# A staged float32 kernel (chunked attention and two feed-forward experts): two column pairs of the last product taken in turn, loads spread, due times on one line

## The chip, the cores and the metric

One core of one Trainium2 chip runs the whole kernel. The metric is the device time of one execution in microseconds (us). Of this kernel three executions were timed; one further execution was recorded by the hardware profiler, and every row below is from that one.

The core's engines run their own queues in order: TensorE (PE; its weight loads are PEld), VectorE (DVE), ScalarE (ACT), GpSimd (POOL) and SyncE (SP, which issues all DMAs here). An instruction at the head of a queue that waits holds everything behind it.

## The reference

Attention within chunks of 64 positions, then two experts on the 4608 resulting rows of 512:

```python
# q, k, v: (8, 8, 576, 64); 9 chunks of 64 positions
scores = scale * np.matmul(q_c, k_c.transpose(0, 1, 2, 4, 3))
attn = np.exp(scores - scores.max(-1, keepdims=True)); attn /= attn.sum(-1, keepdims=True) + 1e-09
x = np.matmul(attn, v_c)                    # reordered to (4608, 512)
# first expert: w_in (512, 1024), w_out (1024, 512)
h = x @ w_in
solu = h * softmax(h)
ln = (solu - mu) / np.sqrt(var + 1e-06) * g_ln
y = ln @ w_out
# second expert: w2_in (512, 2048), w2_out (2048, 512)
h = y @ w2_in
return ((h * sigmoid(h)) @ w2_out).astype(np.float32)
```

Activations are float32, the weights float64 (their bits come in as pairs of int32 words).

## The kernel before

Every product is made of three passes over rounded halves (`PASSES`): high x high, high x low, low x high, in the f32r type. A "split" makes the two halves: ScalarE writes the rounded high part, then VectorE or GpSimd subtracts it (L380, L532, L685).

The stages, in order of time:

1. *Tiles* (L753 on), 36 of 128 rows each: q/k load and transpose, scores, softmax, attention times v, first expert in (`moe_in`, L401), its softmax and normalisation, transposes, and by blocks of four tiles the first expert out (`moe_out`, L461; `y_store`, L469). Between them the weights are converted from float64: `conv_load` (L130, one DMA into one of the two places of tag `st_w`), `conv_a` (L143), `conv_b` (L164), `conv_c` (L187), a chain of VectorE steps with one step of ScalarE.
2. *The second expert's way in*, 24 pairs of units of 14 products (`product`, L571; `PA` = 14.588 on the plan). `w2_in` is used in the seven-product form of a 2 x 2 block product: `w2_mix` (L221) makes the seven sums of each block on GpSimd, splits them and stores them (`w2d`); `t_load` (L486) brings the factors back. The results pass through nine places `tmp` (L548) and are stored to `gd` by `g_store` (L583); a place is free again when its store has landed. Meanwhile `w2_out` is converted and mixed in the same way (L867 to L876), into `w2od`.
3. *The way out*, 18 pairs of row tiles, seven products each (`out_product`, L692; 24 matmuls of 256 columns). `w2o_load` (L637) brings the factors in, 512 KB an issue, into places that the way in gives up; `g_load` (L672) brings the four quarters of a pair; `g_sum` (L676: two sums on VectorE, two on GpSimd), `g_split` (L685: ScalarE, then VectorE for the first four, GpSimd for the last three) into a ring of six places, and `o_p1`, `o_sum`, `o_c11` (L705 to L719) combine and store.

Nothing orders itself. Each step is a generator with a list of due times (`Plan.at`, L35), in microseconds of an ideal time line; `Plan.run` (L40) sorts all steps by due time and emits them in that order, so the due times set only the order within each engine's queue. The first tiles have due times written out by hand in the table `LEAD` (L926), in hundredths: up to tile 13 or 14, from -53.24 to 147.93. What isn't in the table has due times by formulas in `T[t]`, the start of tile t (L729), `Z` (last tile), `XO`, `XA` (way in), `XB` (way out) and `SB` = 2.88, one product of the way out. In the table tile 13's first product is due at 139.18; by the formula before, T[13] is 185.9, so the table's steps all come ahead of the formulas'. `conv_load(18)` is the first conversion that isn't in the table; it is due at T[12] - 13.5.

The lines that the steps below touch: L159 and L160 (the two VectorE instructions of `conv_a`), L250 and L252 (high and low part in `w2_mix`), L356 (the softmax product on GpSimd), L391 (VectorE's part of a split, from PSUM), L596 (`u2` of a unit in the way in, VectorE), L610 (`c22`), L674 (`g_load`), L681 (`g_sum`), L688 and L690 (the split of the way out), L710 (`o_sum`). `p2` accumulates on the bank of `p1` and `p7` takes the bank of `p6`, so those products wait for `o_p1` and `u2` of their pair to have read it (`place`, L558). The plan's part for the first pairs of the way out:

```python
for vp in range(NP):
    x = XB + 7 * SB * vp
...
        if vp < 2:
            y = XB + ((-7.5, -6.0, -3.5, -2.0, 3.5, 5.0, 7.0), (11.8, 13.0, 14.8, 17.6, 19.0, 20.3, 23.3))[vp][o]
        at((y, y + 1.25), g_split, vp, o)
        at(x + o * SB, out_product, vp, o)
```

## Time and profile before

| | before |
|---|---|
| time, median of 3 runs | 1358.24 us (1356.92 to 1359.31) |
| the profiled execution: time / span | 1358.2 / 1356.4 us |
| busy share of the span: PE / DVE / ACT / POOL | 94 / 66 / 45 / 42 % |
| mean granted TensorE clock | 0.985 |
| DMA, mean over the span | 160 GB/s, engines busy 57% |

The views used below: *windows* give, for each stretch, the busy time of every engine with its count of instructions, the granted TensorE clock (1.00 is 2.4 GHz, 0.50 would be 1.2 GHz all through), the share of the 16 DMA engines that was busy and the GB/s moved. The *timeline* gives instructions in order of time, neighbours of one line merged (x12 is twelve of them): start, duration, engine, line, operation, output <- inputs and shapes; a bracket tells how long the engine was idle before it and what released it. SPq rows are DMAs being issued. The *chain of waits* goes back from the last instruction. Times in rows are from the start of the span; the plan's due times are on another scale, and only their order and distances count.

### The profile page before, as it was taken

Reading aid. Unit: us, or ns where it says so; the run is one execution under the profiler, and the core shown is the slowest. Engines: PE = TensorE matmul, PEld = TensorE weight load, DVE = VectorE, ACT = ScalarE, POOL = GpSimd, SP = SyncE. Lnnn points to the kernel's source line nnn. Section 1 sums busy time; section 2 is a strip of 40 time slices with the busy share of each in tenths; the row PEclk is TensorE's granted clock in tenths of the full one; section 3 lists DMA queues with packets and bytes.
Section 4 is the critical chain, followed back from the end, with each engine's and each line's share of the span. In section 5 each row is a group of like instructions: output and inputs, shape, how many; then the busy total and the mean of one; then the engine's idle time right before and its main releaser. Section 6 shows DMA issues by size and latency. Waiting matters only on the chain. (4 is left out here: it accounts for less than half of the span.)

```text
span 1356.4 us, 22472 instructions
## 1 busy us (share of the span) xinstructions
PE 1274.6 (94%) x8400; PEld 1166.2 (86%) x8400; DVE 900.7 (66%) x1383; ACT 609.4 (45%) x991; POOL 568.2 (42%) x454
## 2 busy tenths in 40 slices
PE   3789998999999999999999999998889999999998
PEld 2578886887888788788999999988889999999997
DVE  7799785877888788534656656562566666666661
ACT  5686444544544455433545445342333443333341
POOL 4443112321321332322554556252165666676662
PEclk9999999999999999999999999999899999999999
DMA  9574356656555651877676566749973434443420
GB/s 198 93 136 93 68 113 157 134 110 144 140 105 137 148 125 60 289 257 242 199 231 212 184 204 197 216 153 290 334 278 116 145 121 136 135 129 130 134 90 29
DMA packets 330846, 217.51 MB, mean 160 GB/s; under 512 B 187248, under 2 KB 288624, under 8 KB 330736
## 3 DMA queue, kind: packets, MB, share of 16 engines
q1 hardware_dynamic: 330736, 216.07, 56.8%
q8 instruction: 66, 1.08, 0.3%
q14 instruction: 44, 0.36, 0.1%
HBM read 130.03 MB, written 85.98 MB: 159 GB/s over the span
## 5 line engine op out<-in xcount | busy, mean ns | idle before, releaser
L580 PE MATMUL h<-y1s,w2t 128*128 128x384 f32 x1440 | 264.2, 339 | 14.1 <-DVE tmp L596 7.8
L697 PE MATMUL h<-w2o,gs 128*128 128x256 f32 x2160 | 267.3, 284 | 4.4 <-DVE ob L710 3.4
L580 PEld LDWEIGHTS h<-y1s,w2t 128*128 128x128 f32 x1440 | 254.0, 190 | 17.1 <-DVE tmp L596 9.4
L697 PEld LDWEIGHTS h<-w2o,gs 128*128 128x128 f32 x2160 | 263.6, 193 | 4.8 <-DVE ob L710 3.6
L407 PE MATMUL h<-wi,xs 128*128 128x512 f32 x864 | 218.2, 403 | 5.4 <-DVE u L424 2.5
L466 PE MATMUL yp<-lnT,wo 128*128 128x512 f32 x864 | 211.9, 395 | 0.7 <-ACT ys L471 0.7
L407 PEld LDWEIGHTS h<-wi,xs 128*128 128x128 f32 x864 | 162.3, 192 | 42.9 <-ACT e L346 2.9
L466 PEld LDWEIGHTS yp<-lnT,wo 128*128 128x128 f32 x864 | 159.1, 188 | 38.5 <-issue 5.0
L688 ACT ACTIVATE gs<-g 128x1024 fp32r<-128x1024 f32 x117 | 123.4, 1058 | 145.0 <-PE h L697 76.3
L690 POOL TENSOR_TENSOR gs<-g,gs 128x1024 fp32r<-128x1024 f32 x54 | 146.2, 2711 | 51.4 <-ACT gs L688 47.4
L690 DVE TENSOR_TENSOR gs<-g,gs 128x1024 fp32r<-128x1024 f32 x63 | 105.0, 1667 | 33.8 <-ACT gs L688 33.8
L580 PE MATMUL hw<-y1s,w2t 128*128 128x384 f32 x576 | 111.4, 342 | 4.3 <-DVE tmp L610 4.3
L697 PE MATMUL hw<-w2o,gs 128*128 128x256 f32 x864 | 109.7, 282 | 0.9 <-DVE ob L710 0.6
L580 PEld LDWEIGHTS hw<-y1s,w2t 128*128 128x128 f32 x576 | 103.1, 192 | 6.5 <-DVE tmp L610 6.5
L697 PEld LDWEIGHTS hw<-w2o,gs 128*128 128x128 f32 x864 | 105.8, 191 | 1.7 <-DMA w2o<-w2od 0.9
L434 POOL TENSOR_TENSOR st<-st,nhalf 128x1 f32<-128x1 f32 x36 | 21.2, 590 | 197.4 <-DVE st L432 197.4
L237 POOL TENSOR_TENSOR cv<-cv 128x256 f32<-128x256 f32 x64 | 46.1, 737 | 98.4 <-DVE cv L207 97.2
L391 DVE TENSOR_TENSOR lnT<-tp,lnT 128x512 fp32r<-128x512 f32 x72 | 49.4, 686 | 38.7 <-ACT lnT L382 37.9
L681 POOL TENSOR_TENSOR g<-g,g0x 128x1024 f32<-128x1024 f32 x18 | 43.4, 2412 | 74.7 <-DVE gs L690 74.7
L356 POOL TENSOR_TENSOR e<-e,sm 128x512 f32<-128x512 f32 x36 | 42.1, 1170 | 76.5 <-DVE sm L354 69.9
L382 ACT ACTIVATE lnT<-tp 128x512 fp32r<-128x512 f32 x72 | 42.9, 595 | 64.9 <-PE tp L452 64.9
L596 DVE TENSOR_TENSOR tmp<-h,tmp 128x384 f32<-128x384 f32 x48 | 26.6, 556 | 62.0 <-DMA gd<-tmp 26.8
(116 smaller groups left out, 1810.2 us busy)
## 6 DMA issues: line engine op xcount, KB each, us to landing
gd<-tmp SPq DMA_DIRECT2D x192, 192.0 KB
g<-gd SPq DMA_DIRECT2D x72, 512.0 KB
w2d<-cv_m SPq DMA_DIRECT2D x56, 256.0 KB
w2t<-w2d SPq DMA_DIRECT2D x56, 256.0 KB
w2od<-y1s SPq DMA_DIRECT2D x56, 256.0 KB
w2o<-w2od SPq DMA_DIRECT2D x27, 512.0 KB
st_w<-in_moe_w_out_dram SPq DMA_DIRECT2D x24, 512.0 KB
vt<-in_v_dram SPq DMA_DIRECT2D x36, 256.0 KB
```

The source lines that it names most:

```text
L237: nc.gpsimd.tensor_tensor(out=out, in0=in0, in1=in1, op=op)
L356: nc.gpsimd.tensor_tensor(out=e, in0=e, in1=sm.to_broadcast([128, HP, 2, CH]), op=ALU.mult)
L382: nc.scalar.activation(out=hi, in_=src, func=AF.Copy)
L391: nc.vector.tensor_tensor(out=lo, in0=src, in1=hi.bitcast(F32), op=ALU.subtract)
L407: nc.tensor.matmul(h_t[t][:, n, :], xs[:, a, kk, :], wi[b][kk][:, n * 512:(n + 1) * 512], start=(kk == 0 and i == 0), stop=(kk == KD - 1 a ...
L466: nc.tensor.matmul(yps[b, m], wo[a][f // 4][:, f % 4, 128 * m:128 * (m + 1)], lnT[b][c][:, f, :], start=(f == 0 and i == 0), stop=(f == K1 ...
L580: nc.tensor.matmul(acc, w[:, a, kk, :], t[:, i, c, :], start=start and kk == 0 and n == 0, stop=kk == 1 and n == 2, skip_group_check=not s ...
L596: nc.vector.tensor_tensor(out=c, in0=bank[u, "y"], in1=c_t[u, "p1"], op=ALU.add)
L681: on.tensor_tensor(out=out, in0=in0, in1=in1, op=op_)
L688: nc.scalar.activation(out=dst[:, 0], in_=src, func=AF.Copy)
L690: (nc.gpsimd if o > 3 else nc.vector).tensor_tensor(out=dst[:, 1], in0=src, in1=dst[:, 0].bitcast(F32), op=ALU.subtract)
L697: nc.tensor.matmul(acc, g[:, a, f, :], wo2[o, f][:, c, :], start=start and f == 0 and i == 0, stop=f == NF - 1 and i == 2, skip_group_chec ...
```

## The change

The diff does five things. `T[t]` becomes `L * t - 46.7`, so that the formulas and the table lie on one time line and the steps near tiles 12 to 15 interleave. In `w2_mix` of the way in the four parts are spaced 3.6, 6.9, 13.7, 17.4 instead of evenly by 3.8; `t_load` of the `wo` places goes at half the pace. The conversions of `w2_out` get other places, `conv_a` a break between its two VectorE instructions, and their loads are due 7.0 ahead or 5.3 after the piece before. The factors of the way out are loaded at a slower pace in their second to fourth groups, and the fourth starts later. And the first two pairs of the way out take turns: `turn` gives pair 0 the slots 0, 1, 3, 5, 7, 9, 11 and pair 1 the slots 2, 4, 6, 8, 10, 12, 13; ring, loads, sums, splits and stores of these pairs follow new due times, and the places for the results are given by a fixed table.

```diff
-    def conv_a(i):
+    def conv_a(i, apart=False):
...
         nc.vector.tensor_scalar(out=cv[:, 0, :], in0=hi, scalar1=0x7FF00000, scalar2=None, op0=ALU.bitwise_and)
+        if apart:
+            yield
         nc.vector.tensor_scalar(out=cv[:, 1, :], in0=hi, scalar1=0xFFFFF, scalar2=0x100000, op0=ALU.bitwise_and, op1=ALU.bitwise_or)
...
+    def turn(v, o):
+
+        return 7 * v + o if v > 1 else ((0, 1, 3, 5, 7, 9, 11), (2, 4, 6, 8, 10, 12, 13))[v][o]
...
-        dst = ring[(7 * v + o) % 6]
+        dst = ring[turn(v, o) % 6]
...
-        ob.append(ob.pop(0))
-        o_t[v, name] = ob[-1]
-        return ob[-1]
+
+        if v < 2:
+            n = {"p1": (0, 2), "u2": (1, 3), "u3": (4, 0), "c22": (5, 2)}[name][v]
+        else:
+            n = (1, 4, 5, 2, 0, 3)[len(takes) % 6]
+            takes.append(n)
+        o_t[v, name] = ob[n]
+        return ob[n]
...
-    T = [L * t for t in range(TT + 1)]
+    T = [L * t - 46.7 for t in range(TT + 1)]
...
             at(x - 13.5, conv_load, nxt)
+            x = T[t] + (3.6 if nxt == 18 else 0.0)
             at((x + 2.0, x + 2.6), conv_a, nxt)
...
-                    at([y, y + 0.9, y + 1.8, y + 2.7] + [y + 3.6 + 3.8 * (i // 3) + (0.0, 1.0, 2.6)[i % 3] for i in range(12)], w2_mix, (nxt - 17) // 2, 0)
+                    at([y, y + 0.9, y + 1.8, y + 2.7] + [y + (3.6, 6.9, 13.7, 17.4)[i // 3] + (0.0, 1.0, 2.6)[i % 3] for i in range(12)], w2_mix, (nxt - 17) // 2, 0)
...
-        (XA + 0.1, ("wo", "wo")),
-        (XA + 9.0, ("wo", "wo")),
+        (XA + 0.1, ("wo", "wo", "wo", "wo")),
...
-            at([when + (4.4 if tag == "wo" else 0.01) * i + (1.1 if tag == "wo" else 0.001) * k for k in range(n + 1)], t_load, tag, BUFS.get(tag, 2), n)
+            at([when + (8.8 if tag == "wo" else 0.01) * i + (2.2 if tag == "wo" else 0.001) * k for k in range(n + 1)], t_load, tag, BUFS.get(tag, 2), n)
...
-        x = XA + PA * (8 * (i // 6) + ((0.8, 1.4, 2.5, 4.3, 5.5, 6.1) if i < 6 else (0.5, 1.1, 2.2, 2.75, 5.4, 6.0))[i % 6])
-        at(x - 5.0 if i else XA - 1.0, conv_load, n)
-        at((x, x + 1.2), conv_a, n)
-        at((x + 2.4, x + 3.6), conv_b, n)
-        at(x + 4.8, conv_c, n)
+        x = XA + PA * (8 * (i // 6) + ((0.7, 1.4, 2.4, 4.3, 5.4, 6.1) if i < 6 else (0.4, 1.1, 2.2, 2.85, 5.4, 6.1))[i % 6])
+        at(max(x - 7.0, before + 5.3), conv_load, n)
+        before = x
+        at((x, x + 1.0, x + 2.0), conv_a, n, True)
+        at((x + 3.0, x + 4.0), conv_b, n)
+        at(x + 5.0, conv_c, n)
...
         (XB - 2.98 * PA, 1.15, ("wo", "wo", "wo")),
-        (XB - 1.98 * PA, 0.95, ("wo", "u", "u", "wi", "wi", "wi", "wi")),
-        (XB - 13.6, 0.85, ("wi", "wi", "wi", "wi", "xs", "vt", "vt")),
-        (XB + 0.25, 0.55, ("qr", "qr", "kr", "kr", "kT", "pT", "qT", "e")),
+        (XB - 1.98 * PA, 1.4, ("wo", "u", "u", "wi", "wi", "wi", "wi")),
+        (XB - 6.4, 1.5, ("wi", "wi", "wi", "wi", "xs", "vt", "vt")),
+        (XB + 14.7, 0.95, ("qr", "qr", "kr", "kr", "kT", "pT", "qT", "e")),
...
+    FIRST_LOADS = ((-52.5, -52.3, -52.1, -51.9), (-6.0, 2.4, -4.0, 2.1), (18.5, 21.5, 15.0, 17.0))
+    FIRST_SUMS = ((-9.5, -9.0, -3.0, 6.0), (5.4, 6.4, 9.0, 12.0))
+    FIRST_SPLITS = (-7.5, -6.0, 0.0, -2.0, 7.6, 3.0, 9.0, 11.0, 13.6, 15.5, 17.5, 20.0, 22.0, 24.5)
     for vp in range(NP):
         x = XB + 7 * SB * vp
...
+            n = turn(vp, o)
+            y = XB + (FIRST_SPLITS[n] if n < 14 else (n - 4.7) * SB)
             at((y, y + 1.25), g_split, vp, o)
-            at(x + o * SB, out_product, vp, o)
...
+            at(XB + n * SB, out_product, vp, o)
+            ends.append(XB + n * SB + SB)
+        d = 0.6 if vp == NP - 1 else 3.4
...
+        at((ends[4], ends[4] + d), o_sum, vp, "c22", "w", "u3", 1)
```

(The factor groups are due time, time for each 256 KB unit, places; `before` starts at XA - 6.3. Of the loads of `g_load` before, pair 0's were due at -52.5, -49.6, -46.7 and -43.8 from `XB`, pair 1's at 0.3 to 2.4, pair 2's at 11.0 and just after. Some due times of `raw_t` and of the mixing of `w2_out` move by a few us.)

## Rows read from the trace of the kernel before

**Rows 1.** Windows: from:to, length, busy us (instructions) of each engine, clock, DMA share, GB/s
```profile
605.00:617.00 12.00, 12.00 (x71) 12.00 (x70) 6.74 (x13) 4.66 (x10) 0.00 (x0) 1.00 0.94 286
...
925.00:975.00 50.00, 42.55 (x234) 41.57 (x232) 19.69 (x31) 14.42 (x29) 6.15 (x8) 0.97 1.01 344
...
1025.00:1050.00 25.00, 25.00 (x212) 25.00 (x211) 15.74 (x15) 10.09 (x11) 15.97 (x7) 1.00 0.33 111
```

**Rows 2.** The chain of waits: start, us, what; around the way out
```profile
985.04 8.82 DMA g<-gd
...
1102.86 2.88 PE h L697 x24
```

**Rows 3.** Timeline: start, us, engine, line, instruction [idle before, releaser]; the seam
```profile
210.46 1.28 POOL L252 TENSOR_TENSOR cv_m<-cv,cv_m 128x512 fp32r<-128x512 f32 x1
...
219.14 2.91 PE L407 MATMUL h<-wi,xs 128*128 128x512 f32 x12
...
225.81 1.04 SPq L140 DMA_DIRECT2D st_w<-in_moe_w_in_dram  x2
...
230.51 0.43 DVE L159 TENSOR_SCALAR cv<-st_w 128x512 int32<-128x512 int32 x1 [7.57 <-DMA st_w<-in_moe_w_in_dram]
...
233.66 0.68 DVE L391 TENSOR_TENSOR lnT<-tp,lnT 128x512 fp32r<-128x512 f32 x1
...
234.40 1.12 PE L452 MATMUL tp<-ident,u 128*128 128x128 f32 x4 [6.01 <-DVE lnT L391]
...
241.42 2.91 PE L407 MATMUL h<-wi,xs 128*128 128x512 f32 x12
...
256.05 2.91 PE L407 MATMUL h<-wi,xs 128*128 128x512 f32 x12
```

**Rows 4.** Timeline, all engines: tile 18, and the wait of its twin, tile 28
```profile
300.12 2.91 PE L407 MATMUL h<-wi,xs 128*128 128x512 f32 x12
...
307.14 0.42 ACT L250 ACTIVATE cv_m<-cv 128x256 fp32r<-128x256 f32 x1 [4.86 <-DMA w2d<-cv_m]
...
309.42 0.97 PE L362 MATMUL pp<-ident,e 128*128 128x128 f32 x4 [3.23 <-POOL e L356]
...
319.61 2.91 PE L407 MATMUL h<-wi,xs 128*128 128x512 f32 x12
...
459.60 0.97 PE L362 MATMUL pp<-ident,e 128*128 128x128 f32 x4 [2.09 <-POOL e L356]
```

**Rows 5.** Timeline, TensorE: the first pairs of the expert's way in
```profile
623.70 3.88 PE L580 MATMUL h<-y1s,w2t 128*128 128x384 f32 x12 [1.68 <-DVE tmp L596]
```

**Rows 6.** Timeline: the middle of the way in
```profile
764.06 3.84 POOL L517 TENSOR_TENSOR ry<-ry 128x768 f32<-128x768 f32 x2
...
766.12 2.06 DVE L160 TENSOR_SCALAR cv<-st_w 128x512 int32<-128x512 int32 x1
...
896.64 6.00 PE L580 MATMUL h<-y1s,w2t 128*128 128x384 f32 x24 [2.80 <-ACT tmp L592]
```

**Rows 7.** Timeline: the last pairs of the way in
```profile
950.19 0.56 DVE L596 TENSOR_TENSOR tmp<-h,tmp 128x384 f32<-128x384 f32 x1 [6.74 <-DMA gd<-tmp]
...
950.81 1.89 PE L580 MATMUL h<-y1s,w2t 128*128 128x384 f32 x6 [3.84 <-DVE tmp L596]
...
974.94 3.91 PE L580 MATMUL hw<-y1s,w2t 128*128 128x384 f32 x12 [2.47 <-DVE tmp L610]
```

**Rows 8.** Timeline: the first two pairs of the way out
```profile
978.69 11.66 PE L697 MATMUL h<-w2o,gs 128*128 128x256 f32 x96
...
1009.23 3.28 DVE L681 TENSOR_TENSOR g<-g 128x1024 f32<-128x1024 f32 x1 [4.48 <-DMA g<-gd]
...
1014.16 5.49 PE L697 MATMUL h<-w2o,gs 128*128 128x256 f32 x24 [3.42 <-DVE ob L710]
```

**Rows 9.** Costliest groups: line, engine, shapes, count | busy us, mean ns | idle before
```profile
L688 ACT ACTIVATE gs<-g 128x1024 fp32r<-128x1024 f32 x117 | 123.4, 1058 | 145.0 <-PE h L697 76.3
...
L690 DVE TENSOR_TENSOR gs<-g,gs 128x1024 fp32r<-128x1024 f32 x63 | 105.0, 1667 | 33.8 <-ACT gs L688 33.8
```

More of the change, by code (lines that the diff above doesn't have):

```diff
@@ L634, in chunk_attention_moe_moe @@
     NP = TT // 2
-    wo2, wu, ring, raw_g, op, ob, o_t = {}, [], [], {}, {}, [], {}
+    wo2, wu, ring, raw_g, ob, takes, o_t = {}, [], [], {}, [], [], {}
     def w2o_load(tag, bufs, n):
@@ L657, in g_places @@
         elif n == 4:
-            for i in (2, 3):
+            for i in (0, 2):
                 raw_g[1, i] = sb.tile([128, NF, 128], F32, tag="cv", name="g1", bufs=2)
         elif n == 5:
-            for i, tag in ((0, "cv_s"), (1, "cv_s"), (4, "st_w")):
+            for i, tag in ((3, "cv_s"), (1, "cv_s"), (4, "st_w")):
                 raw_g[1, i] = sb.tile([128, NF, 128], F32, tag=tag, name="g1", bufs=2)
@@ L693, in out_product @@
         acc, start = place(1000 + v, SEVEN[o], 256)
-        g = ring[(7 * v + o) % 6]
+        g = ring[turn(v, o) % 6]
         for f in range(NF):
@@ L898, in chunk_attention_moe_moe @@
         for i in (2, 3, 0, 1):
[L899 to L900 removed]
+            at(XB + FIRST_LOADS[vp][i] if vp < 3 else x - 11 * SB + 0.1 * i, g_load, vp, i)
         for n in range(4):
[L902 to L905 removed]
+            at(XB + FIRST_SUMS[vp][n] if vp < 2 else x + (-6.2, -5.7, -3.2, -0.9)[n] * SB, g_sum, vp, n)
+        ends = []
         for o in range(7):
[L907 to L909 removed]
+            n = turn(vp, o)
+            y = XB + (FIRST_SPLITS[n] if n < 14 else (n - 4.7) * SB)
             at((y, y + 1.25), g_split, vp, o)
[L911 to L919 removed]
+            at(XB + n * SB, out_product, vp, o)
+            ends.append(XB + n * SB + SB)
+        d = 0.6 if vp == NP - 1 else 3.4
+        at(ends[0], o_p1, vp)
+        at(ends[1], o_sum, vp, "u2", "y", "p1", 1)
+        at((ends[2], ends[2] + d), o_c11, vp)
+        at(ends[3], o_sum, vp, "u3", "y", "u2", 1)
+        at((ends[4], ends[4] + d), o_sum, vp, "c22", "w", "u3", 1)
+        at((ends[5], ends[5] + d), o_sum, vp, "c21", "v", "u3", 0)
+        at((ends[6], ends[6] + d), o_sum, vp, "c12", "w", "u2", 0)
     with tc.manual_schedule(engines={ET.PE, ET.SP, ET.Activation, ET.DVE, ET.Pool}):
```

24 lines of the change are left out of this document (4 added, 20 removed).

## Prediction

> **What bounds the kernel now.** I read the engines' busy time first (the table above): TensorE is busy 94% of the span, so only its idle time and its slow-clock time can be won. Then the windows: in the steady way out TensorE works in every microsecond, 212 matmuls in 25 us at a granted clock of 1.00 [rows 1]; nothing can be gained there. Then the timeline of TensorE alone for each wait above 0.3 us, and the other engines around each. A wait costs its own length and, where the clock fell from 2.4 to 1.2 GHz in it, the extra time of the next matmuls. Full speed is 0.169 us for a matmul of 384 columns (71 in 12.00 us) and 2.88 us for 24 of 256 [rows 1, 2]. After the first 100 us, where no queue's order changes, the losses lie in six places:
>
> (a) The seam, where the hand-written lead table ends. Tile 13 starts at 219.14, tile 14 at 241.42: 22.28 us, where the next takes 14.63. Loss 7.6. VectorE stood 7.57 us at `conv_a(18)`, whose load SyncE issued only at 225.81; the split that frees the transposes' bank queued behind it, and TensorE waited 6.01 [rows 3].
> (b) Tiles 18 and 28, each after an odd tile with a `w2_mix`, whose stores queue on SyncE behind the q/k loads. ScalarE stood 4.86 us for such a store to land, GpSimd's subtraction behind it, and the softmax product behind that on GpSimd; TensorE waited 3.23 and the tile took 19.49, 4.9 too many. The twin's wait was 2.09; with the same slow clock (4.86 - 3.23) that is 3.7. Loss 8.6 [rows 4].
> (c) The start of the expert's way in: two waits of this kind (one row stands), 1.52 and 1.68, with 0.3 and 1.9 of slow clock. Loss 5.4 [rows 5].
> (d) Its middle: two waits of one shape (the second stands), 1.65 and 2.80, with 0.4 and 1.9 of slow clock. Loss 6.8 [rows 6].
> (e) Its end: the 50 us from 925 hold 234 matmuls, 39.5 us of work, so 10.5 are lost, and 1.9 more to the slow clock after 974.94. Loss 12.4 [rows 1, 7].
> (f) The first pairs of the way out: ten products take 35.5 us (978.69 to 1014.16) instead of 28.8, with a wait of 3.42 at the end, and the next one 5.49 instead of 2.88 by the slow clock. Loss 9.3 [rows 2, 8].
>
> That is 50 us in all.
>
> **The change part by part.** No arithmetic is added or removed and all 8400 matmuls stay; TensorE's own order changes only in the first 14 products of the way out. What moves is the place of other instructions in their queues.
>
> *One time line (a).* T is 46.7 less, so `conv_load(18)` falls at 111.4, inside the lead table, some 28 places earlier on SyncE, and `conv_a(18)` at 130.5. The load's place is free after `conv_b(16)`, due at 116.0; until 119.2 nothing else is due on SyncE, so holding that queue costs nothing. But `conv_a(18)` also needs the `cv` that the second part of `w2_mix(0)` leaves at 211.74, and its chain, 3.15 us from the first instruction to the split behind it, then sits ahead of that tile's split, transposes and maximum instead of in an empty stretch [rows 3]. ScalarE and TensorE wait for those. I take 3 us lost where 7.6 were (0 to 5): gain 4.6 (2.6 to 7.6). `load_qk(9)` now stands ahead of a `y_store` on SyncE; the two places of `ys` cover the delay, a tile's length.
>
> *Parts of `w2_mix` (b).* The third part moves 2.5 later, its subtraction behind GpSimd's softmax product, which is due 0.9 after the old place and 1.6 before the new. ScalarE still waits until about 307, but TensorE then has the next half of its tile to do. Gain 7.5 (0 to 8.6).
>
> *`t_load` of the last 16 factors (c).* 16 x 256 KB come in 35 us instead of 17.6, 119 GB/s instead of 238, in a stretch that ran at 286 [rows 1]. The stores whose landing frees `tmp` get through sooner. The last factor is due 33.1 into the stage and first used at about 57. Gain 4 (1 to 5.4).
>
> *Conversions of `w2_out` (d).* Half of the loads go out 7.0 instead of 5.0 ahead of their use, the others 4.2 to 4.9, and `conv_a`'s two instructions have places apart. In both waits VectorE stood for the load and then worked beside GpSimd's two subtractions: L160 took 2.06, where its sister L159 takes 0.43 alone [rows 3, 6]. Now `c21` goes ahead of the two and `c12` soon behind, so what is left delays neither for long. I take 5 of 6.8 (1 to 6.8). The Trainium skill, SBUF — State Buffer, section Who interferes with whom, says that such a VectorE instruction and a GpSimd one shut each other out fully. The rows agree: 2.06 ends as the second subtraction does. By that rule each of the two, now apart, could be held up for 1.9, the gain would be 3, and the sum 2 us later.
>
> *Loads before the way out (e).* By the diff's due times, 512 KB a load: the second group left each 1.9 us (276 GB/s), now each 2.8 (187); the third each 1.7 (308), now each 3.0 (175). The `gd` stores add eight of 192 KB in 14.6 us, 108. So the demand falls from 384 and 416 to 295 and 283, where the DMA engines, all busy, moved 344 [rows 1]. The `gd` store for which VectorE stood 6.74 us lands sooner, and TensorE's 3.84 and 0.9 go [rows 7]. The wait at 974.94 is VectorE's own work for the first splits; GpSimd's first sum stands 2 later and may halve it. Against it, the first pair's four loads leave in one burst at -52.5: 2.1 MB at 344 GB/s hold the queue for 6 us, which can cost 0 to 4; I take 1.5. Gain 6 (1 to 10).
>
> *Two pairs in turn (f).* Pair 0 has slots 0, 1, 3, 5, 7, 9, 11, pair 1 has 2, 4, 6, 8, 10, 12, 13. The last factor is first used at 31.7 instead of 17.3. The old wait goes: VectorE's first sum of pair 2 stood 4.48 us for its load ahead of `u2` of pair 1, which is now due 8 earlier than that sum [rows 8]. A new one comes: slot 4 needs pair 1's sums and so its a22. That load follows the store of `c12(47)`, as the old one did; then it began 6.3 after the stage and took 8.82 [rows 2]; now perhaps 4.0, and 4.7 as the pair of loads at 225.81 did [rows 3]. Two sums, ScalarE's pass and VectorE's take 3 x 1.67 + 1.06 = 6.1 [rows 9]. Slot 4 is ready between 14.8 and 21.2 against 11.5, or up to 2 sooner where VectorE isn't held up: a wait of 1 to 10, taken as 3, with 2.6 of slow clock. It shifts the later slots alike and is paid once. Gain 9.3 - 5.6 = 3.7 (-3 to 8). Output stores leave 2.8 later; the six `ob` places leave 8 us before one is needed again.
>
> Sum: 4.6 + 7.5 + 4 + 5 + 6 + 3.7 = 30.8; the low ends sum to 3, the high ones to 46. The profiled execution took 1358.2 (its span 1356.4 and 1.8 around it), which is the median of the runs, so 1358.2 - 30.8 = **1327**.
>
> **Rivals.** *Only the tiles.* The queue still carries, from plan time -7.3 to 11.6 around the start of the way out, six factor loads, four of products and six stores: 6.4 MB in 18.9 us, 340 GB/s, as much as the 344 of the full stretch [rows 1]. If it stays full, (e) and (f) give nothing together and (c) and (d) half: 4.6 + 7.5 + 4.5 = 16.6, 1342. For it: that demand; against: the 30 us before it are well below. The Trainium skill, DMA: Bandwidth & Descriptors, section Specifications, gives some 358 GB/s of HBM for one core; by it 340 would just pass.
>
> *All of it.* (a) and (b) whole, (c) and (d) whole, (e) 10, (f) 8: 46, 1312. For it: each wait was released by an instruction that the diff moves. Against: the late a22.
>
> *The turns starve* (slower). With two pairs open at once, every slot from 4 to 13 waits for its split, as GpSimd falls behind and SyncE holds the last factor loads behind a load that waits for one of its splits. A wait like that at 1014.16 costs 3.42 + 2.6 = 6.0 [rows 8]; ten cost 60 where 9.3 were lost: 1358 - 27 - 9 + 60 = 1382. It makes the kernel slower from seven of the ten slots on. Against it: in the steady pairs GpSimd is busy 15.97 of 25 us [rows 1].
>
> *No change.* The dues move, but landing times set (b) to (f) all the same; then only what is left of (a) stays, within 2.7 us: 1356.
>
> **How the numbers follow.** Forecast (1317 to 1337): 0.62. Only the tiles (1337 to 1352): 0.18. All of it (1306 to 1317): 0.10. No change: 0.04. Starved: 0.06. The range leaves out the last two, half of "all of it" and the far end of "only the tiles": 1314 to 1346. A measurement of this kernel tells about 0.2%, 2.7 us, from no change: faster 0.90, the same 0.04, slower 0.06.
>
> **What would show it.** After: no stand of VectorE for the load of `conv_a(18)`, tile 13 under 18 us; no wait for the softmax product in tiles 18 and 28; no 6 us stand for a `gd` store in the last pairs of the way in; the way out within 370 us, with one wait, at its fifth product. Wrong would be: waits at several of the first fourteen products, one above 5 us in the lead table's last tiles, or a stop some 45 us before the way out, after the four loads in one burst.

## The result, and the profile after

The changed kernel takes 1346.97 us (median of four runs, 1344.13 to 1347.89) against 1358.66 (1356.92 to 1359.31) for the one before in the same comparison: a ratio of 0.9912, 95% interval 0.9895 to 0.9930. That is 11.7 us faster where I had forecast 31, and 1 us above the range. The profiled execution's span is 1345.2 us (1356.4 before), and the spans' difference, 11.2, can be laid out by stage from the first matmul of each:

| stretch | before, us | after, us | gain | predicted |
|---|---|---|---|---|
| up to tile 11's first product | 189.91 | 190.67 | -0.8 | 0 |
| (a) tiles 11 to 14 | 66.14 | 62.00 | 4.1 | 4.6 |
| (b) tile 15 to the way in | 343.17 | 337.24 | 5.9 | 7.5 |
| (c), (d), (e) the way in | 379.47 | 375.36 | 4.1 | 15 |
| (f) the way out | 370.96 | 373.35 | -2.4 | 3.7 |
| what follows | 6.75 | 6.59 | 0.2 | 0 |

So the tiles did nearly what I said, the way in a quarter of it, and the way out the opposite. The way in can be counted by its 24 pairs: a pair is 84 matmuls, which at 0.173 us each (twelve in 2.08 us where TensorE works through) take 14.56 us, and what it takes beyond that is lost. The first four pairs, (c), lost 6.6 before and lose 8.8 now; the 17 behind them, (d), 11.9 and 6.3; the last three, (e), 11.5 and 10.9.

The timeline of TensorE alone shows where. Columns as in [rows 3]; line numbers of the changed kernel are 2 larger than before from the second instruction of `conv_a` to `g_sum`, and 6 to 11 larger behind it (L582 is the way in's matmul, L703 the way out's).

```profile
222.54 3.27 PE L409 MATMUL h<-wi,xs 128*128 128x512 f32 x12 [0.85 <-DVE u L426]
238.10 2.91 PE L409 MATMUL h<-wi,xs 128*128 128x512 f32 x12
...
297.00 2.91 PE L409 MATMUL h<-wi,xs 128*128 128x512 f32 x12
...
312.36 3.26 PE L409 MATMUL h<-wi,xs 128*128 128x512 f32 x12 [0.22 <-DVE u L426]
...
466.47 0.66 PE L364 MATMUL pp<-ident,e 128*128 128x128 f32 x4 [0.35 <-POOL e L358]
...
613.35 3.58 PE L582 MATMUL h<-y1s,w2t 128*128 128x384 f32 x12 [2.44 <-DVE tmp L598]
...
632.78 1.32 PE L582 MATMUL h<-y1s,w2t 128*128 128x384 f32 x6 [1.89 <-DVE tmp L598]
...
639.99 2.37 PE L582 MATMUL hw<-y1s,w2t 128*128 128x384 f32 x12 [1.70 <-DVE tmp L612]
...
937.70 2.29 PE L582 MATMUL h<-y1s,w2t 128*128 128x384 f32 x6 [4.88 <-DVE tmp L598]
...
961.73 3.75 PE L582 MATMUL hw<-y1s,w2t 128*128 128x384 f32 x12 [2.08 <-DVE tmp L612]
...
980.03 11.33 PE L703 MATMUL h<-w2o,gs 128*128 128x256 f32 x70 [2.04 <-DVE gs L696]
...
1005.10 1.34 PE L703 MATMUL hw<-w2o,gs 128*128 128x256 f32 x9 [0.86 <-DMA w2o<-w2od]
1009.08 0.62 PE L703 MATMUL hw<-w2o,gs 128*128 128x256 f32 x3 [2.64 <-DMA w2o<-w2od]
1009.54 4.52 PE L703 MATMUL h<-w2o,gs 128*128 128x256 f32 x24
```

Against [rows 3, 4]: tile 13 now takes 15.56 us (222.54 to 238.10) where it took 22.28, tile 18 takes 15.36 (297.00 to 312.36) where it took 19.49, and the twin's wait is 0.35 where it was 2.09. Against [rows 5]: the start of the way in still stops, now three times. Against [rows 7]: the wait for VectorE's `u2` near the end is not gone but longer, 4.88 for 3.84. Against [rows 8]: the old wait at 1014.16 is gone, and in its place stand the one that I had forecast at the fifth product (980.03) and two for factors, which I had not.

### The profile page after: what moved, and what is told of

It is laid out like the page before. It is cut to its first block, busy times and chain, and to the rows that moved or that the text cites. A ratio compares the mean times of both kernels' runs of the same rounds, so it can differ in the third digit from the quotient of the medians.

```text
span 1345.2 us, 22475 instructions
## 1 busy us (share of the span) xinstructions
PE 1271.6 (95%) x8400; PEld 1162.0 (86%) x8400; DVE 898.2 (67%) x1383; ACT 609.7 (45%) x991; POOL 567.1 (42%) x454
## 3 DMA queue, kind: packets, MB, share of 16 engines
q8 instruction: 66, 1.08, 0.3%
## 5 line engine op out<-in xcount | busy, mean ns | idle before, releaser
L703 PE MATMUL h<-w2o,gs 128*128 128x256 f32 x2160 | 269.4, 286 | 2.5 <-DVE gs L696 2.0
L582 PE MATMUL h<-y1s,w2t 128*128 128x384 f32 x1440 | 261.6, 337 | 9.9 <-DVE tmp L598 9.2
L703 PEld LDWEIGHTS h<-w2o,gs 128*128 128x128 f32 x2160 | 265.8, 194 | 3.1 <-DVE gs L696 2.2
L582 PEld LDWEIGHTS h<-y1s,w2t 128*128 128x128 f32 x1440 | 252.4, 189 | 11.8 <-DVE tmp L598 10.4
L409 PEld LDWEIGHTS h<-wi,xs 128*128 128x128 f32 x864 | 159.4, 190 | 45.8 <-issue 3.2
L582 PE MATMUL hw<-y1s,w2t 128*128 128x384 f32 x576 | 111.6, 343 | 6.8 <-DVE tmp L612 6.8
L703 PE MATMUL hw<-w2o,gs 128*128 128x256 f32 x864 | 109.2, 282 | 3.5 <-DMA w2o<-w2od 3.5
L582 PEld LDWEIGHTS hw<-y1s,w2t 128*128 128x128 f32 x576 | 103.3, 193 | 9.1 <-DVE tmp L612 9.1
L703 PEld LDWEIGHTS hw<-w2o,gs 128*128 128x128 f32 x864 | 105.5, 191 | 3.9 <-DMA w2o<-w2od 3.9
L598 DVE TENSOR_TENSOR tmp<-h,tmp 128x384 f32<-128x384 f32 x48 | 26.6, 556 | 63.1 <-DMA gd<-tmp 34.7
```

The lines of the kernel that those rows point to most:

```text
L409: nc.tensor.matmul(h_t[t][:, n, :], xs[:, a, kk, :], wi[b][kk][:, n * 512:(n + 1) * 512], start=(kk == 0 and i == 0), stop=(kk == KD - 1 a ...
L582: nc.tensor.matmul(acc, w[:, a, kk, :], t[:, i, c, :], start=start and kk == 0 and n == 0, stop=kk == 1 and n == 2, skip_group_check=not s ...
L598: nc.vector.tensor_tensor(out=c, in0=bank[u, "y"], in1=c_t[u, "p1"], op=ALU.add)
L703: nc.tensor.matmul(acc, g[:, a, f, :], wo2[o, f][:, c, :], start=start and f == 0 and i == 0, stop=f == NF - 1 and i == 2, skip_group_chec ...
```

## What held VectorE and SyncE

The waits of the way in, seen from VectorE and SyncE's queue (a timeline of the changed kernel, both ends of the stage; L598 is `u2`, L590 a store of `tmp` to `gd`, L257 a store of the mixing of `w2_out`):

```profile
606.93 0.38 SPq L140 DMA_DIRECT2D st_w<-in_moe_w_out_dram  x1
607.40 0.40 SPq L590 DMA_DIRECT2D gd<-tmp  x1
...
612.74 1.02 DVE L598 TENSOR_TENSOR tmp<-h,tmp 128x384 f32<-128x384 f32 x2 [5.81 <-DMA gd<-tmp]
...
626.35 1.00 SPq L590 DMA_DIRECT2D gd<-tmp  x2
...
632.17 0.56 DVE L598 TENSOR_TENSOR tmp<-h,tmp 128x384 f32<-128x384 f32 x1 [4.82 <-DMA gd<-tmp]
...
927.99 0.32 SPq L257 DMA_DIRECT2D w2od<-y1s  x1
928.40 0.96 SPq L590 DMA_DIRECT2D gd<-tmp  x2
...
930.30 1.88 SPq L590 DMA_DIRECT2D gd<-tmp  x3
...
937.09 0.56 DVE L598 TENSOR_TENSOR tmp<-h,tmp 128x384 f32<-128x384 f32 x1 [7.78 <-DMA gd<-tmp]
```

Each of these three waits is for a store that had only just been issued: 607.40 to 612.7, 626.35 to 632.2, and 931.64 (the third of the three merged at 930.30) to 937.1, so 5.3 to 5.8 us of landing. (The start's third stop, 1.70 at 639.99, is of another kind: VectorE's conversion came late behind a mixing step of GpSimd, which had stood 7.66 for a store of the mixing.) Which store it is follows from `take`. There are nine places and each pair of units takes eight, handed round in the order of taking. So `u2` of a pair's second unit gets the place that `u2` of the first unit held in the pair before, and that one is given up late, by the store of `c12`: on the plan 4.0 us earlier. In the second pair, where two of the nine places have joined the list late, `u2` of the first unit gets a place whose store was due 2 us earlier. No pace of the loads gives such a store more than 4 us to land. In my prediction I never asked how long the order of the places leaves for it.

In the way out (timeline of VectorE and SyncE, then the chain of waits, then a window with columns as in [rows 1]):

```profile
973.65 1.23 DVE L683 TENSOR_TENSOR g<-g,g 128x1024 f32<-128x1024 f32 x1 [1.73 <-DMA g<-gd]
...
979.90 0.64 SPq L734 DMA_DIRECT2D out_dram<-ob  x1
985.93 0.33 SPq L676 DMA_DIRECT2D g<-gd  x1
986.35 0.38 SPq L646 DMA_DIRECT2D w2o<-w2od  x1
```
```profile
999.26 9.77 DMA w2o<-w2od
```
```profile
980.00:985.00 5.00, 4.97 (x23) 4.97 (x24) 1.11 (x1) 1.85 (x3) 3.81 (x2) 0.50 0.14 45
```

From 980.54 to 985.93 SyncE issued nothing, and the DMA engines moved 45 GB/s: its next instruction was pair 2's load into a place that a split of pair 0, on GpSimd until about that time, still read. The last seven issues of factors stood behind it and its three fellows; the last landed at 1009.03, in the middle of the twelfth product.

## The experiments

In all of them the kernel before, in the same comparison, took 1355.8 to 1358.6 us. A kernel's time moved by several us between runs there, so I read mostly the stages' lengths in the traces, one for each kernel. They have a spread of their own: four kernels whose instructions in the way in stand in the same order (the changed one, `factors_first`, `split_stores` and, but for one load and the last pair, `turns_undone`) took 375.4, 374.9, 376.5 and 372.7 us for it, and three with the same way out (the changed one, `conv_undone`, `old_pace`) 373.4, 374.4 and 374.8. The table has them all; "tiles" is tile 11's first product to the way in.

| kernel | time, us (range) | tiles | way in | way out |
|---|---|---|---|---|
| before | 1358.66 | 409.3 | 379.5 | 371.0 |
| changed | 1346.97 | 399.2 | 375.4 | 373.4 |
| tiles_only | 1349.65 (1345.56-1356.63) | 398.9 | 383.0 | 370.4 |
| places_released | 1336.68 (1335.78-1338.46) | 399.0 | 365.5 | 375.6 |
| factors_first | 1342.39 (1340.16-1344.95) | 398.5 | 374.9 | 369.4 |
| turns_undone | 1341.85 (1339.34-1342.25) | 398.9 | 372.7 | 369.3 |
| released_old_pace | 1333.20 (1330.40-1334.77) | 398.6 | 361.2 | 376.1 |
| conv_undone | 1353.71 (1350.54-1355.97) | 399.1 | 381.6 | 374.4 |
| factor_pace_undone | 1345.87 (1344.43-1346.51) | 398.2 | 378.7 | 368.7 |
| released_in_order | 1332.91 (1329.82-1334.63) | 398.5 | 363.0 | 370.1 |
| old_pace | 1345.67 (1343.87-1346.08) | 398.3 | 373.9 | 374.8 |
| all_mended | 1326.18 (1323.53-1326.33) | 398.9 | 360.2 | 369.3 |
| later_turns | 1331.87 (1331.10-1333.21) | 398.9 | 362.7 | 373.1 |
| in_order_mended | 1326.67 (1324.74-1330.21) | 398.5 | 359.6 | 368.3 |
| later_mended | 1324.64 (1323.47-1326.32) | 398.9 | 361.4 | 367.1 |
| later_early_stores | 1327.99 (1326.26-1332.22) | 398.6 | 361.4 | 370.2 |
| split_stores | 1337.13 (1336.73-1337.44) | 398.5 | 376.5 | 367.1 |
| later_split | 1320.26 (1318.15-1322.38) | 399.0 | 361.2 | 363.9 |
| in_order_split | 1322.99 (1322.12-1324.35) | 398.7 | 361.8 | 367.6 |

**The tiles alone.** The kernel before with `T` shifted by 46.7, 3.6 on `conv_a(18)`, and the new spacing of `w2_mix`.

> The kernel before with the tile part of the change alone: the one time line for T, conv_a(18) 3.6 later, and the new spacing of w2_mix's four parts. Theory (each part of the change pays for itself): read from the two traces, the changed kernel gains 4.1 us at the seam and 5.9 in the tiles behind it, 10.1 in all, so this should take 1358.4 - 10.1 = 1348, and the way in and the way out should last as before, 379.5 and 371.0 us. Rival (the later parts are coupled to the tiles, since the tiles' last steps shift the loads of the way in): the way in alone changes by more than 2 us and the time lies outside 1346 to 1350.

Ratio 0.9946 (0.9924 to 0.9968). The tiles take 398.9 us, so (a) and (b) stand by themselves, 10.4 us. But the way in took 383.0, 3.6 more than before, which the rival had, though the time stays inside its 1346 to 1350. Part of it is the clock after the stop at the start (granted 0.72 and 0.94 in the twenty us from 608.84, 0.83 and 1.00 in the same twenty of before), 1.3 a wait of 1.85 at 805.36 which was 0.52. Both were there before, only shorter. The way in has its instructions in the same order in both kernels, and 3.6 is no more than the four kernels above differ by, so a coupling to the tiles is not shown.

**The order of the places.** In the way in, a place goes to the end of the list when it is stored:

```diff
     def take():
-        tmp.append(tmp.pop(0))
-        return tmp[-1]
+        return tmp.pop(0)
...
         nc.sync.dma_start(out=gd[...], in_=c.rearrange("p (t c) -> p t c", c=128))
+        tmp.append(c)
```

> The changed kernel, but a place tmp of the way in goes back to the end of the list when its store is issued, not when it is taken. With nine places and eight taken in each pair of units, the order of taking gives u2 of the second unit the place whose c12 store was due 4.0 us before on the plan, and in the second pair, where two places come late, u2 gets one whose store was due 2 us before; the order of release leaves at least 8 us for every place. Theory (the waits at the start and the end of the way in, 2.44, 1.89 and 4.88 with 2.3 and 1.5 of slow clock, are the short time that this order leaves for a store to land, and loads at another pace can't take them away): all three go or shrink below 0.5, and the time falls by 9 to 12 us, to 1335 to 1338. Rival (the DMA queue is full in these stretches and VectorE waits for it whatever the place): the waits stay, at other products, and the time is within 3 us of the changed kernel's 1347.

The way in fell by 9.8 us to 365.5 and the kernel to 0.9854 (0.9827 to 0.9881) of before, as the theory had it: the waits of 2.44, 1.89 and 4.88 are gone. By the count of pairs 8.5 of the 9.8 come from the last three pairs (2.4 lost where 10.9 were) and only 1.6 from the first four (7.2 where 8.8 were). Timeline of VectorE (line numbers in the way in are one smaller here), and windows, of the end of its way in:

```profile
928.46 0.56 DVE L598 TENSOR_TENSOR tmp<-h,tmp 128x384 f32<-128x384 f32 x1 [2.40 <-DMA gd<-tmp]
```
```profile
922.00:927.00 5.00, 5.00 (x31) 5.00 (x30) 1.58 (x3) 1.86 (x4) 1.14 (x2) 1.00 1.01 345
927.00:932.00 5.00, 5.00 (x30) 5.00 (x29) 1.28 (x3) 0.99 (x2) 0.00 (x0) 1.00 1.08 293
```

The DMA engines are as full as in the changed kernel (1.01 and 1.08) and TensorE works through: the queue was not the cause, the time left for the store was. VectorE still stands 2.40 for a store, which costs nothing now. One stop at the start grew, from 1.70 to 3.90 (timeline of the same kernel): VectorE's conversion waits for a mixing step of GpSimd, and that for a store of the mixing to land.

```profile
627.86 0.40 POOL L250 CAST y1s<-cv 128x256 fp32r<-128x256 f32 x1 [7.69 <-DMA w2od<-y1s]
...
629.11 0.59 DVE L159 TENSOR_SCALAR cv<-st_w 128x512 int32<-128x512 int32 x1 [6.92 <-POOL y1s L254]
...
633.83 2.61 PE L581 MATMUL hw<-y1s,w2t 128*128 128x384 f32 x7 [3.90 <-DVE tmp L612]
```

**The pace of the last 16 factors**, first on top of that, then alone; both have `("wo", "wo")` at `XA + 0.1` and at `XA + 9.0` and 1.1 us a unit again.

> The kernel with the places in the order of release, and the last 16 factors of the way in (t_load into wo) at the pace of the kernel before, 1.1 a unit in two groups. In the kernel at the slow pace one wait is left at the start of the way in: 3.90 at 633.83, where VectorE's conv_a had stood 6.92 for a mixing step of GpSimd, which stood 7.69 for a store of w2od to land. Theory (the slow pace drags the factor loads into the stretch from 618 to 632, where the mixing's stores, raw_load's four loads and a conversion's load are on the queue too; the pace was the wrong thing to change): that wait falls below 1, nothing takes its place, and the way in takes 360 to 362 us instead of 365.5. Rival (the stretch is full at either pace): the way in takes 364 to 368.

> The changed kernel with t_load's last 16 factors at the pace of the kernel before; nothing else. My prediction gave this pace 4 us. Theory (at the start of the way in the order of the places sets the stop, and the pace only moves it from the first pairs to the third): the start loses 5.5 to 8.5 us at either pace, and the way in takes within 2.5 us of the 375.4, 374.9 and 372.7 of the three kernels with the slow pace. Rival (my prediction): without the slow pace the way in takes 378 to 380.

With the places mended the old pace is better by 4.3 us (way in 361.2): the stop at 633.83 shrinks to 1.98, though not below 1. With the places as they are the pace changes nothing: 373.9 against 372.7 to 376.5, with waits of 1.60, 1.94, 0.76 and 1.01 in place of 2.44, 1.89 and 1.70. So the slow pace of the change is at best worth nothing.

**The conversions of w2_out**, due as before, loads and mixing too.

> The changed kernel with the conversions of w2_out as in the kernel before: due times of the loads, of conv_a to conv_c and of the mixing, and conv_a's two instructions together. Theory (my prediction's step for the middle of the way in, 5 us, was right: the two traces show 10.0 of waits and slow clock there before and 4.8 after): waits of 1.6 to 2.9 at p1 of the pair come back twice in the middle, and the way in takes 379 to 382 us instead of 375.4. Rival (the middle was freed by what happens ahead of it, not by these due times): the way in stays within 1.5 us of 375.4.

The way in took 381.6, 6.3 more, nearly all of it in the middle (12.5 lost there where 6.3 were), with the two waits of [rows 6] back at the same places (TensorE's timeline; 1.65 and 2.80 before):

```profile
769.38 4.46 PE L582 MATMUL h<-y1s,w2t 128*128 128x384 f32 x24 [1.59 <-ACT tmp L594]
...
893.84 6.00 PE L582 MATMUL h<-y1s,w2t 128*128 128x384 f32 x24 [2.87 <-ACT tmp L594]
```

**The pairs in order, and the factors' pace at the end of the way in.** `turns_undone` has `turn` as `7 * v + o` and the due times, places and last two factor groups of before; `factor_pace_undone` has in addition

```diff
-        (XB - 1.98 * PA, 1.4, ("wo", "u", "u", "wi", "wi", "wi", "wi")),
+        (XB - 1.98 * PA, 0.95, ("wo", "u", "u", "wi", "wi", "wi", "wi")),
...
-            y = XB + FIRST_LOADS[0][0] if vp == 0 else ...
+            y = XB - (3.6 - 0.2 * i) * PA if vp == 0 else ...
```

> The changed kernel with the first two pairs of the way out one after the other, as in the kernel before: their slots, sums, splits, loads and places, and the third and fourth group of factors, as before; pair 0's loads in one burst, the second group's slow pace and all that is ahead of the way out stay changed. Theory (the turns cost more than they bring, since the last factors land too late): the way out takes 371 us as before, and the kernel 2 us less than the changed one, 1345. Rival (my prediction: the turns bring some 4 us by themselves): 1350 to 1352.

> The changed kernel with its way out in order (as the kernel turns_undone), and in addition the second group of w2_out's factors at the old pace (0.95 a unit) and pair 0's four loads 2.9 us apart as before. With that the end of the way in is as it was before the change. Theory (the stop there is the 4.0 us that the order of the places leaves for c12's store to land, and the queue is full at either pace): the wait for u2 of the second unit, 3.46 in turns_undone, stays between 2.5 and 5, and the way in takes 372 to 375 us against 372.7 there. Rival (my prediction: the pace is worth 6 us): 377 to 380 us.

In order, the way out takes 369.3, 4.0 less than with the turns: as built, with the late factors that came with them, they cost 4 us. The pace together with the burst of pair 0's loads is worth 6.0 against `turns_undone` (378.7 and 372.7), as I had said, and there my later theory missed. But against the other three of that order it is only 2.2 to 3.8, and in the last three pairs alone, where the edit acts, 13.8 are lost against 9.2 to 10.9. The wait for `u2` (TensorE's timelines, `factor_pace_undone`, then `turns_undone`):

```profile
938.50 2.29 PE L582 MATMUL h<-y1s,w2t 128*128 128x384 f32 x6 [6.64 <-DVE tmp L598]
```
```profile
934.16 1.32 PE L582 MATMUL h<-y1s,w2t 128*128 128x384 f32 x6 [3.46 <-DVE tmp L598]
```

The slower pace does land the store sooner; with 4.0 us on the plan that isn't soon enough.

**The factors ahead of pair 2's loads.**

```diff
-        (XB + 14.7, 0.95, ("qr", "qr", "kr", "kr", "kT", "pT", "qT", "e")),
+        (XB + 4.0, 0.75, ("qr", "qr", "kr", "kr", "kT", "pT", "qT", "e")),
```

> The changed kernel, but the last group of w2_out's factors (qr to e, 14 units) is due at XB + 4.0 in steps of 0.75 instead of XB + 14.7 in steps of 0.95, so that SyncE issues all of it ahead of the loads of pair 2. Theory (SyncE stood until 985.93 for the place of pair 2's load, which a split of pair 0 reads, and held the factor loads behind it; the last of them landed at 1009.03): the waits of 0.86 and 2.64 in the twelfth product and their slow clock go, 5 us, and the way out takes 368 us instead of 373; 1342. Rival (the DMA engines can't bring 3.5 MB more before then, and the transfers collide): the same wait stands at another product or for pair 2's loads, the way out takes 372 to 375 us, 1347.

The waits for factors went, and the way out takes 369.4, 3.9 less. A new one came, for an `ob` place whose store took 10.73 us to land (chain of waits, TensorE's timeline, and a window in those 10.73):

```profile
1004.68 10.73 DMA out_dram<-ob
```
```profile
1015.96 5.99 PE L703 MATMUL h<-w2o,gs 128*128 128x256 f32 x48 [2.31 <-ACT ob L717]
```
```profile
1008.00:1010.00 2.00, 2.00 (x19) 2.00 (x18) 2.00 (x3) 0.93 (x1) 2.00 (x1) 1.00 0.14 48
```

The engines were nearly idle while it took so long: 0.14 busy, 48 GB/s. This comes back below.

**Together, with and without turns.** `released_in_order` joins the release order and the pairs in order; `all_mended` joins release order, old pace, factors first and `(5, 4, 2, 1, 0, 3)` for the `ob` places; `in_order_mended` joins release order, old pace, the pairs in order, and `(-4.6, -4.2, -3.2, -0.9)` for pair 2's sums.

> The changed kernel with the places of the way in in the order of release and the way out in order. If the two gains are independent, the way in takes 365.5 us less some 2 (turns_undone's was 2.6 shorter than the changed kernel's, by its third group of factors) and the way out 369.3: 1331 us. If the earlier end of the way in only moves the wait for the factors (the way out of places_released was 2.3 longer than that of the changed kernel), the way out takes 372 and the kernel 1334.

> The changed kernel with places in the order of release, t_load at the old pace, the last factor group ahead of pair 2's loads, and the ob places handed on in the order in which the first two pairs free them (5, 4, 2, 1, 0, 3). If the terms add up: the way in takes 361 us (released_old_pace), the way out 366 to 369 (369.4 in factors_first less its wait of 2.31 for an ob place; one wait of 2 and its slow clock left at the fifth product), the kernel 1325. If the end of the way in, now 14 us earlier against the loads, lacks the transfers (released_old_pace's way out took 376.1), waits for w2o stay and the way out takes 371 to 375: 1329 or more.

> Places in the order of release, t_load at the old pace, the way out in order with its old due times but for VectorE's two sums of pair 2, which are due 4.6 us later, behind u2 of pair 1. Theory (in order, the loss at the eleventh product is VectorE standing for pair 2's load ahead of u2): that wait (2.21 in released_in_order) goes with its slow clock, what is left is the wait for the last factors (2.87), and the way out takes 366 to 368 us, the kernel 1325 to 1328. It also tells whether turns are needed at all: if all_mended is not faster than this, taking turns brought nothing that a sum in another place doesn't bring.

`released_in_order` lies between its two cases, way out 370.1, with a wait of 2.87 for factors at 972.90: an end of the way in that comes earlier meets the factors earlier. `all_mended` and `in_order_mended` end level, 0.9768 (0.9751 to 0.9785) and 0.9781 (0.9759 to 0.9802) of before, both 1.3 to 1.5% faster than the changed kernel. In the first, the fifth product waits 3.33 and 1.73, and its chain of waits says why (then TensorE's timeline):

```profile
947.04 7.27 DMA gd<-tmp
...
954.37 5.46 DMA g<-gd
```
```profile
963.69 0.80 PE L703 MATMUL h<-w2o,gs 128*128 128x256 f32 x2 [3.33 <-ACT gs L694]
```

The way in's last store must land before pair 1's load of it may go: 12.7 us for the two, and the slot begins about 11.5 after the start of the way out.

**Pair 1 two slots later.** `turn` as `((0, 1, 2, 3, 5, 7, 9), (4, 6, 8, 10, 11, 12, 13))` with sums and splits to match; then the same with its new waits taken away, and once more with early stores. (In `later_turns` a sum of pair 1 runs ahead of the split that still reads its place, so one low half is made from the wrong numbers, by the same instructions; the two others have it in the right order.)

> As all_mended, but pair 1 comes in later: pair 0 has the slots 0, 1, 2, 3, 5, 7, 9, pair 1 the slots 4, 6, 8, 10 to 13; sums and splits are due accordingly. Theory (the wait at the fifth product is the turns' own: pair 1's p6 needs a22, whose load can only follow c12's last store): the wait goes, the way out takes 4 to 5 us less than in all_mended, 363 to 365, and the kernel 1321. Rival (the last factors are needed two slots sooner, at the tenth product, and aren't there): a wait for w2o of 2 to 4 us takes its place, and the way out is as long as all_mended's.

> As later_turns, with three things set right: the second sum of GpSimd for pair 1 stands behind the split that reads its a12 (in later_turns it ran ahead of it, so that one low half was made from the wrong numbers, with the same instructions); c22 of pair 1 takes the ob place that c22 of pair 0 left, not the one whose store of c11 was 8.6 us old (7.08 lost there); VectorE's two sums of pair 2 are due behind c22 of pair 0 (2.47 lost there). Theory (taking turns can bring what I predicted, once loads, places and sums leave it room): no wait above 1 us in the first fourteen products, the way out takes 363 to 365 us against 369.3 in all_mended and 368.3 in in_order_mended, and the kernel 1320 to 1322. Rival (the transfers themselves set the end of the first pairs): the wait comes back as one for w2o or for g, the way out takes 367 to 371, 1324 to 1328.

> As later_mended, with the stores of out due 0.6 behind their sums as in the kernel before, instead of 3.4. Theory (a store issued early lands early, and SyncE holds nothing behind it for long, since the loads of the steady pairs need not go out before them): the way out is within 1 us of later_mended's. Rival (SyncE stands for each store's sum, and the loads queued behind it come later): 1 to 4 us more, with waits for g in the pairs 2 and 3.

The wait at the fifth slot went in all three, and no wait for factors came. `later_turns` lost 2.47 to VectorE's sums of pair 2 and 7.08 to an `ob` place; `later_mended` got rid of both, only to wait 3.80 in the twelfth product for pair 2's loads, which now land late behind the factors (its chain of waits, and TensorE's timeline):

```profile
961.37 10.55 DMA w2o<-w2od
...
971.98 8.96 DMA g<-gd
```
```profile
984.90 4.50 PE L703 MATMUL hw<-w2o,gs 128*128 128x256 f32 x24 [3.80 <-DVE ob L721]
```

Its DMA engines moved 304, 369, 417, 398 and 364 GB/s in the five windows of 5 us from 955, busy all through. So the rival seemed to hold: the way out, 367.1, is inside its 367 to 371, and only 1.1 below the pairs in order. Early stores moved the wait to 6.40 and the way out to 370.2, as their rival had it: the change's later stores are worth 3 us where two pairs are open.

**The stores to out.** Left open was why an `ob` place came back so late. `o_store` issues one transfer for two batch rows; here it is two, one for each:

```diff
-        nc.sync.dma_start(out=out...[2 * tt:2 * tt + 2, b * CH:(b + 1) * CH, 256 * n:256 * n + 256], in_=c)
+        rows = out.rearrange("(b s) f -> b s f", b=B)
+        for h in range(2):
+            nc.sync.dma_start(out=rows[2 * tt + h, b * CH:(b + 1) * CH, 256 * n:256 * n + 256], in_=c[CH * h:CH * h + CH])
```

> factors_first, with each store to out issued as two, one for each of its two batch rows (64 partitions, 64 KB). In factors_first the first result of pair 2 waited for a place whose store took 10.73 us, while the DMA engines were 0.14 busy and moved 48 GB/s for 8 us: not behind loads, but behind other stores, four of 128 KB. Theory (a store over two batch rows is cut in two and uses 2 of 16 engines; 0.14 x 16 = 2.2): cut along its 64 rows instead, a store goes over all engines, the windows without loads no longer stand at 48 GB/s, the wait of 2.31 at 1015.96 goes with its slow clock of 0.2, and the way out takes 366 to 367.5 us against 369.4. Rival (rows of 1 KB written to memory go at 48 GB/s however they are cut): the window and the wait stay, 369 to 370.

> later_mended with the stores to out split in the same way. If the stores' engines matter to the loads in flight too (two engines carry the stores and their share of each load, so a load lands when those two are done), pair 2's loads land sooner than the 8.96 us there, the wait of 3.80 shrinks and the way out takes 363 to 366 us; if only bytes count, the wait stays within 1 us of 3.80 and the way out is 366 to 368.5.

> in_order_mended with each store to out issued as two, as in later_split. Theory (in order, the last factors are needed at the seventh product, and their landing, not the stores, sets the wait of 2.86; the turns bring what the prediction gave them, some 4 us, once the stores are out of their way): the wait for w2o stays above 2, the way out takes 366.5 to 368.5 us, and later_split, at 363.9, is 3 to 4.5 us ahead. Rival (the split stores help both alike): 363 to 365.5, and the turns bring less than 1.5.

`split_stores` took 1337.13 us, and its way out 367.1, 2.4 less than `factors_first`; the wait for `ob` is gone. The end is shorter too, which I had not asked for: from the last matmul to the end of the span pass 4.0 us instead of the 6.6 of `factors_first`, in this kernel and in the two below. Its ten half stores from 1001.76 to 1012.75 landed after these times (the view of `o_store`'s line):

```profile
DMA to landing us min/median/max: 2.0/3.2/7.7
```

The longest stood behind four loads. In `factors_first` the engines had kept at 0.14 and 48 GB/s for eight us on end. So the slow store was the transfer's form and not its rows of 1 KB, which are the same. That it was 2 of 16 engines is worked out from 0.14 x 16 = 2.2, not seen engine by engine.

With the turns it matters more. `later_split`'s chain of waits and TensorE's timeline, then the timeline of `in_order_split`:

```profile
961.14 10.31 DMA w2o<-w2od
...
971.51 6.71 DMA g<-gd
```
```profile
983.99 3.11 PE L703 MATMUL hw<-w2o,gs 128*128 128x256 f32 x24 [1.90 <-DVE ob L721]
```
```profile
970.29 0.98 PE L703 MATMUL h<-w2o,gs 128*128 128x256 f32 x6 [2.74 <-DMA w2o<-w2od]
```

Pair 2's load lands after 6.71 instead of 8.96, the wait shrinks from 3.80 to 1.90, and the way out takes 363.9. In order, the factors are late for the sixth product whatever the stores do, and the way out takes 367.6. By these traces, one of each kernel, the turns are worth 3.8, as I had said of them, but only in this form: with the release order, pair 1 later and the stores split, none of which the prediction had. The timings do not resolve it: 0.9734 (0.9709 to 0.9758) of before with the turns, 0.9733 (0.9701 to 0.9765) in order, each beside its own runs of before. Either is some 1.8% faster than the changed kernel.

## Why the prediction was wrong, point by point

- *(a) the seam, 4.6: right.* 4.1, tile 13 under 18 us, no stand of VectorE for `conv_a(18)`'s load.
- *(b) the tiles, 7.5: right*, a little high: 5.9. Both waits for the softmax product are down to 0.35 or nothing.
- *(c) the start of the way in, 4 (1 to 5.4): wrong, and this step failed most.* 8.3 are lost there now (6.0 in the three waits, 2.3 of slow clock) where 5.4 were (8.8 and 6.6 by the count of pairs). The step said "the stores whose landing frees `tmp` get through sooner". But a store that the order of places leaves 2 or 4 us to land needs 5 to 6 beside a conversion's load of 512 KB and factors of 256 KB at any of the two paces, and the slower pace carries the factors on into the next pairs. `places_released` took two of the three waits away, `old_pace` none. What is left there hangs on the stores of the mixing, and it takes both, the release order and the old pace, to bring the loss down to 4.2.
- *(d) the middle, 5 (1 to 6.8): right.* From 650 us on to the last pairs 10.0 us of waits and slow clock became 4.8 (11.9 and 6.3 by the count of pairs), and undoing it costs 6.3. By the rule that I cited from the Trainium skill, SBUF — State Buffer, section Who interferes with whom, the gain would have been 3. The rule itself still holds in the trace: the timeline shows L162, the second of `conv_a`'s two, at 0.42 alone and at 0.96 beside a subtraction of GpSimd. Set apart, though, the two no longer met one long enough to matter.

```profile
614.01 0.42 DVE L162 TENSOR_SCALAR cv<-st_w 128x512 int32<-128x512 int32 x1
...
635.78 0.96 DVE L162 TENSOR_SCALAR cv<-st_w 128x512 int32<-128x512 int32 x1
```

- *(e) the end of the way in, 6 (1 to 10): the term too big by far.* The 12.4 was 0.9 too high to begin with, since the 71 matmuls that I read in 12.00 us [rows 1] count two that reach over its ends; twelve in a row take 2.08 us:

```profile
600.34 2.24 PE L582 MATMUL h<-y1s,w2t 128*128 128x384 f32 x12
602.42 2.25 PE L582 MATMUL hw<-y1s,w2t 128*128 128x384 f32 x12
```

  By that, 10.9 are lost where 11.5 were, a gain of 0.6. The pace does act, as `factor_pace_undone` shows (2.9 to 4.6 in the last three pairs), but that kernel loses more there than the kernel before, 13.8 to 11.5; what in the rest of the change takes the difference back I did not test. My step compared a demand of 295 GB/s with the 344 of the full stretch and called the queue relieved. But the windows around the wait show them full at less, or at little more:

```profile
930.00:935.00 5.00, 2.82 (x17) 2.50 (x15) 0.00 (x0) 0.49 (x1) 0.00 (x0) 1.00 1.03 291
935.00:940.00 5.00, 2.30 (x7) 2.30 (x8) 1.11 (x2) 0.49 (x1) 0.00 (x0) 0.50 1.01 352
```

  Also, SyncE issued `c22`'s stores only at 928.40, behind a mixing store (L257, 927.99) whose data GpSimd had finished at 927.96, and the store on which `u2` hung only at 931.64, 5 us after ScalarE had finished its data. The burst of pair 0's loads, which I had charged with 1.5, did no harm: no wait stands between it (900 to 903) and 937.
- *(f) the turns, 3.7 (-3 to 8): wrong.* The price of the fifth product was right: 0.36 and 2.04 of waits and 2.9 of slow clock, 5.3, for my 5.6. The term left out is the last factors: 3.5 of waits and 2.1 of slow clock. I had seen SyncE hold them "behind a load that waits for one of its splits", but only as part of the rival in which every slot starves, and given that rival 0.06. As a single hold it costs what the turns had gained and 1.6 more (the way out lost 2.4 in all). `factors_first` shows it: 3.9 back. The gain that I had forecast for the turns, 3.7, exists in the traces of `later_split` against `in_order_split`; what stays unsettled is whether timing would confirm it.

The rivals: "only the tiles" gave a time, 1342, near the measured one, but not for its reason: (d) came whole, and (c) and (f) turned negative. Of the signs that I had listed as wrong, waits at several of the first fourteen products came (the fifth and the twelfth), the stop after the burst did not. And two of the signs that I had named for being right stayed away: VectorE stood 7.78 us for a `gd` store in the last pairs, and the way out took more than 370 us.

## What to carry to other kernels

Before a transfer is put at another pace, ask how much time the plan leaves between the store of a buffer and its next use: handing buffers on in the order of release instead of the order of taking lengthened the shortest such time on the plan from 2 us to 8 (but for one place in the first pair, 4) and brought 9.8 us, where with the new paces the start and the end of the way in together had gained nothing (-2.2 and 0.6). When a load must wait for a buffer on a queue that issues in order, list what stands behind it and when each of those is first used. And when a stage ends earlier, the loads for the next stage are missed earlier; a gain ahead of a full queue is partly paid back behind it.

## What the runs showed of the hardware

Where stores to `out` stood alone on the queue, they ran at 48 GB/s with the DMA engines 0.14 busy, so that one of 128 KB behind others took 10.73 us (`factors_first`); issued by batch row they landed in 3.2 us (median of ten halves), loads beside them landed sooner too, and the end of the span came 2.5 us sooner after the last matmul. I had read those 48 GB/s in no window, since the steady way out hides them. A load of 512 KB took 5 us from issue to landing where little stood ahead of it (968.67 to 973.63 in the changed kernel) and 9.8 to 10.6 where the engines were full. The Trainium skill, DMA: Bandwidth & Descriptors, section Specifications, gives some 358 GB/s for one core, as its half of a stack. Here the measurement decides: the windows show up to 417 in 5 us (`later_mended`, from 965), but 306 over the 40 us from 925 in the changed kernel, where the queue carried the 192 KB stores of `tmp` among its loads.
